# A cluster attention kernel: scores against the centroids from the tile of k and q, a transfer that adds, and a new order of the work

## The chip, the core and the metric

The kernel runs on one core of a Trainium2 chip. The metric is the device time of one execution in microseconds (us), the median of several runs of the same program.

## The reference

Attention over 32 heads (4 batches of 8) of 768 rows and 64 columns, in which a query sees only those keys that fall into its own cluster of 16; then a gated linear unit over the 512 columns of the 8 heads of a batch: a causal convolution of width 5 makes the gate.

```python
q_assign = np.argmax(np.einsum('bhsd,hcd->bhsc', q_n, c_n), axis=-1)
k_assign = np.argmax(np.einsum('bhsd,hcd->bhsc', k_n, c_n), axis=-1)
mask = q_assign[:, :, :, None] == k_assign[:, :, None, :]
scores = scale * np.matmul(q, k.transpose(0, 1, 3, 2))
scores = np.where(mask, scores, -1000000000.0)
attn = np.exp(scores - np.max(scores, axis=-1, keepdims=True))
attn = attn / (np.sum(attn, axis=-1, keepdims=True) + 1e-09)
x = np.matmul(attn, v)
# x as (batch, 768, 512), then
for k in range(5):
    gate_pre += conv_w[k][None, None, :] * xp[:, k:k + S, :]
out = (1.0 / (1.0 + np.exp(-gate_pre)) * (x @ w_val)) @ w_out
```

## The kernel before, in words

**Heads and tiles.** Heads are taken in 16 pairs. For a head, the scores stand transposed: a tile has 128 keys on the partitions and 768 queries along a row, so a head has 6 key tiles. Four matmuls make one (L614, L619): k and q are split into a high and a low part, and the two matmuls per half of the queries share one buffer `sp` of two in PSUM. The mask takes part in the matmul: 16 rows of the operands hold the cluster of each key and, times 2^100, that of each query, so that scores of other clusters come out far below zero. ScalarE takes the exponential of a tile (`expo`, L642) into one of 16 buffers `pt`, with a shift that VectorE finds from the head's first tile (L633, L637). TensorE multiplies v by the tiles of both heads of a pair (`av`, L759), 12 steps for a pair.

**Sums.** The denominator is the sum over all keys. VectorE first adds the six tiles of a head into one buffer `ad` of two (`add_p`, L213 by the helper `both`): five additions of 128x768 in f32 for each head. TensorE then sums over the partitions for both heads (`sum_p`, L685), which frees the two `ad`. ScalarE copies the sums out (L692), and after a reciprocal and a broadcast through DRAM VectorE scales the output of the pair by them (`scale_x`, L775).

**Clusters.** For each pair, four matmuls against the pair's centroids `cenT` (`prep_sims`, L489) make scores of k and q: 32 rows for each of four blocks. They read tiles `sraw` of their own, 128 x 384, with the 64 columns of both heads on the partitions (`load_sims`, L477). VectorE transposes, takes the largest and transposes back (L499, L510, L511, L512), TensorE finds the first of equal ones (L520), and ScalarE writes a row of ones and zeros (`prep_first2`, L524) and then the mask tile `oht` (`prep_oh`, L529), whose rows are moved to where the matmul operands need them (`prep_mask`, L575, L578). From pair 2 on, two pairs make one group: one `oht` of 768 columns serves four heads.

**Operands.** `load_both` (L415) brings k and q of one head into a tile `raw` of two, k on the even and q on the odd partitions. ScalarE or VectorE rounds to the high part (L217 or L219), VectorE subtracts (L213), and four moves between tiles of SBUF (L428) make four operands.

**The rest.** The weights are decoded from 64-bit floats by VectorE and ScalarE early on (L339 to L347). For each batch, the convolution (L790), the gate (L795), the value projection (`val`, L834, three matmuls a step) and the output projection (`proj`, L865) follow when the four pairs of that batch are through.

**The order.** Every engine has one queue in program order. The code makes a list of about 2,000 operations with what each has to follow and which buffer it takes, and a table of numbers (`PLAN`) gives the one order in which they are issued. An entry may name the engine (V or A) and a buffer's number; `w45` is 45 idle matmuls. All DMAs are issued by SyncE (SP). GpSimd has only work at the start and two instructions at the end.

## Time and profile before

| | us |
|---|---|
| median of 3 runs (461.29 to 463.9) | 463.62 |
| the profiled execution | 462.52 |
| its span, first to last instruction | 460.8 |
| VectorE busy | 408.2 |
| ScalarE busy | 289.2 |
| DMA, share of the 16 engines | 50.8% |

Busy time is the union of an engine's instructions. TensorE's matmuls overlap and their ends are modelled, so its busy share says only that it has something to do; the distance from start to start of two matmuls tells its pace. The span is 1.7 us shorter than the execution's time.

### The profile page before, as it was taken

The page shows a single profiled execution, that of the slowest core. Times are in us where ns is not written, and L with a number is a line of the kernel's source. Part 1 is how long each engine was busy: PE and PEld are TensorE (multiplying, and loading weights), DVE is VectorE, ACT ScalarE, POOL GpSimd, SP SyncE. Part 2 cuts the span into 40 slices and gives each one's busy share as a digit, 9 for nine tenths or more (in the row PEclk, how much of TensorE's full clock was granted, in tenths as well). Part 3 has the DMA queues.
Part 4 walks back from the last instruction along what each step waited for, and adds up shares of the span by engine and source line. Part 5 has one row for each costly group of instructions (what it writes and reads, how often), then busy time and mean ns, then how long its engine had stood idle before and what let it go on. Part 6 is the DMA issues. An engine that isn't in the chain of part 4 may idle for free. (4 is left out here: it accounts for less than half of the span.)

```text
span 460.8 us, 7572 instructions
## 1 busy us (share of the span) xinstructions
PE 448.9 (97%) x2655; PEld 322.1 (70%) x2655; DVE 408.2 (89%) x724; ACT 289.2 (63%) x428; POOL 6.0 (1%) x36
## 2 busy tenths in 40 slices
PE   7899999999999999999999999999999999999996
PEld 6655465655695868648496884958668696848985
DVE  5999899999999999999999798997988886788850
ACT  7968676969794776738964643756657454531521
POOL 4000000000000000000000000000000000000000
PEclk9999999999999999999999999999999999999999
DMA  8666786777567464366545643665435331200112
GB/s 250 219 197 211 226 263 195 245 236 241 174 208 238 142 212 147 126 191 200 181 148 184 215 135 123 183 192 190 158 122 183 133 101 58 68 15 1 70 48 94
DMA packets 39622, 75.17 MB, mean 163 GB/s; under 512 B 10652, under 2 KB 18716, under 8 KB 39580
## 3 DMA queue, kind: packets, MB, share of 16 engines
q1 hardware_dynamic: 39580, 74.65, 50.8%
q8 instruction: 22, 0.36, 0.3%
q14 instruction: 20, 0.16, 0.1%
HBM read 41.60 MB, written 6.38 MB: 104 GB/s over the span
## 5 line engine op out<-in xcount | busy, mean ns | idle before, releaser
L642 ACT ACTIVATE pt<-sp,sp 128x768 f32<-128x768 f32 x192 | 165.7, 901 | 64.9 <-DVE sp L637 25.5
L759 PE MATMUL acc<-pt,vt 128*64 128x384 f32 x768 | 130.0, 490 | 0.0
L213 DVE TENSOR_TENSOR ad<-ad,pt 128x768 f32<-128x768 f32 x128 | 119.9, 951 | 2.1
L614 PE MATMUL sp<-op,op 128*128 128x384 f32 x372 | 102.2, 355 | 3.0 <-ACT pt L642 2.3
L759 PEld LDWEIGHTS acc<-pt,vt 128*64 128x64 f32 x768 | 52.8, 137 | 67.4 <-issue 63.5
L619 PE MATMUL sp<-op,op 128*128 128x384 f32 (+1 forms) x372 | 95.4, 337 | 0.0
L614 PEld LDWEIGHTS sp<-op,op 128*128 128x128 f32 x372 | 63.3, 188 | 28.7 <-ACT pt L642 14.0
L790 DVE SCALAR_TENSOR_TENSOR gate<-xr,cw,gate 128x768 f32<-128x768 f32 (+1 forms) x84 | 67.9, 820 | 2.1 <-ACT gate L217 1.3
L619 PEld LDWEIGHTS sp<-op,op 128*128 128x128 f32 (+1 forms) x372 | 67.3, 188 | 0.2 <-issue 0.2
L865 PE MATMUL acc<-wh_o,h 128*128 128x512 f32 x144 | 50.3, 397 | 0.0
L834 PE MATMUL acc<-xh,wh_v 128*128 128x384 f32 x112 | 38.0, 340 | 0.0
L834 PE MATMUL acc<-xl,wh_v 128*128 128x384 f32 x112 | 37.8, 337 | 0.0
L834 PE MATMUL acc<-xh,wl_v 128*128 128x384 f32 x112 | 37.7, 337 | 0.0
L213 DVE TENSOR_TENSOR ad<-pt,pt 128x768 f32<-128x768 f32 x32 | 30.2, 944 | 2.2 <-ACT pt L642 2.2
L865 PEld LDWEIGHTS acc<-wh_o,h 128*128 128x128 f32 x144 | 27.1, 188 | 5.8 <-issue 0.6
L871 ACT ACTIVATE ob<-acc 128x512 f32<-128x512 f32 (+1 forms) x22 | 12.6, 576 | 29.1 <-PE acc L865 23.8
L213 DVE TENSOR_TENSOR op<-raw,op 128x768 fp32r<-128x768 f32 (+2 forms) x34 | 30.5, 902 | 0.1
L865 PE MATMUL acc<-wl_o,h 128*128 128x512 f32 x72 | 28.6, 397 | 0.0
L692 ACT ACTIVATE lr<-acc 128x384 f32<-128x384 f32 x16 | 7.9, 493 | 24.3 <-PE acc L685 18.5
L840 DVE SCALAR_TENSOR_TENSOR gate<-gate,acc 128x384 f32<-128x384 f32 x28 | 15.4, 549 | 8.6 <-PE acc L834 8.6
L217 ACT ACTIVATE op<-raw 128x768 fp32r<-128x768 f32 x26 | 21.9, 844 | 1.5 <-DMA raw<-kT 0.9
L834 PEld LDWEIGHTS acc<-xh,wh_v 128*128 128x128 f32 x112 | 21.0, 188 | 0.9 <-issue 0.6
(164 smaller groups left out, 490.8 us busy)
## 6 DMA issues: line engine op xcount, KB each, us to landing
op<-op SPq DMA_DIRECT2D x120, 192.0 KB, 2.5
raw<-kT SPq DMA_DIRECT2D x32, 192.0 KB, 3.4
raw<-qT SPq DMA_DIRECT2D x32, 192.0 KB
vt<-v SPq DMA_DIRECT2D x16, 384.0 KB, 4.4
out_dram<-ob SPq DMA_DIRECT2D x23, 256.0 KB, 2.2
sraw<-kT SPq DMA_DIRECT2D x30, 192.0 KB, 3.2
sraw<-qT SPq DMA_DIRECT2D x30, 192.0 KB, 3.8
rs<-rr SPq DMA_DIRECT2D x30, 192.0 KB, 3.3
```

Of the source, the lines that this page charges most:

```text
L213: (V if on[0] == "V" else G).tensor_tensor(out_, a, b, op=op)
L217: S.activation(out_, in_, AF.Copy, scale=x)
L614: PE.matmul(sp[:, hf, 0:HALF], x1[:, ts_], y1[:, hf * HALF:(hf + 1) * HALF], start=True, stop=False)
L619: PE.matmul(sp[:, hf, 0:HALF], x2[0:KR, ts_], y2[0:KR, hf * HALF:(hf + 1) * HALF], start=False, stop=True)
L642: S.activation(o.rearrange("p (a b) -> p a b", a=2), sp[:, :, 0:HALF], AF.Exp, bias=shift[h], scale=QS)
L692: S.activation(lr, lacc.pop(p)[:, 0:HALF], AF.Copy)
L759: PE.matmul(acc[e * D:(e + 1) * D, 0:HALF], vt[:, j, e * D:(e + 1) * D], pts[2 * p + e, j][:, hf * HALF:(hf + 1) * HALF], start=(j == 0), ...
L790: V.scalar_tensor_tensor(g, xr[:, k + c0:k + c1], cw[:, ct, k:k + 1], g, op0=ALU.mult, op1=ALU.add)
L834: PE.matmul(macc["v", b, ch, m][:, 0:HALF], a[:, kt, ms], x[:, kt, cs], start=(kt == 0 and i == 0), stop=(kt == NC - 1 and i == 2))
L840: V.scalar_tensor_tensor(gv, gv, 1.0, macc.pop(("v", b, ch, m))[:, 0:HALF], op0=ALU.add, op1=ALU.mult)
L865: PE.matmul(macc[b, ch, t, c0][:, 0:c1 - c0], x[kt][:, ts_], a[:, kt, c0:c1], start=(kt == 0 and i == 0), stop=(kt == NC - 1 and i == 2))
L871: S.activation(ob[:, 0:c1 - c0], acc[:, 0:c1 - c0], AF.Copy)
```

## The change

Scores against the centroids are taken from `raw`, the tile with k and q of one head on alternate partitions, and the tiles `sraw` with their 60 loads go. For that a second form of the centroids is made at the start: `cen2` has each centroid twice, once on the even partitions (zero on the odd) and once the other way, by one matmul of a copy `cen_d` and two scalings (`spread_cen`). The four blocks of scores are now two heads by two halves. Every pair is a group of its own, so `oht` has 384 columns, and a mask of a head takes two moves of half the width. `raw` has four buffers in place of two.

The last of the five additions of heads 0 to 11 is no longer VectorE's: GpSimd issues a transfer from the last `pt` to `ad` that adds to what is there (`add_last`). `PLAN` is another table.

```diff
@@ -263,6 +263,29 @@
             G.memset(t[r:r + C], 0.0)
 
 
+    oh_s2 = const.tile([P, 1], F32, name="oh_s2")
+    oh_b2 = const.tile([P, 1], F32, name="oh_b2")
+
+    def make_rows():
+        for t, x, y in ((oh_s2, BIG, 1.0), (oh_b2, -BIG, 0.0)):
+            G.memset(t, x)
+            for r in range(0, P, 32):
+                G.memset(t[r:r + C], y)
+
+
+    par = const.tile([P, 2], F32, name="par")
+    V.tensor_reduce(out=par, in_=ident.rearrange("p (a j) -> p j a", j=2), op=ALU.add, axis=AX.X)
+    cen2 = const.tile([P, HB, 2, C], F32, name="cen2")
+    cen_d = const.tile([P, D, 2], F32, name="cen_d")
+    cen_2 = []
+
+    def spread_cen(j):
+        if j is None:
+            cen_2.append(bank())
+            PE.matmul(cen_2[0][:, 0:P], cen_d.rearrange("p d j -> p (d j)"), ident, start=True, stop=True)
+        else:
+            scaled(cen2[:, :, j, :], cen_2[0][:, 0:P].rearrange("p (h c) -> p h c", c=C), par[:, j:j + 1])
+
     cen_f = const.tile([P, D], F32, name="cen_f")
     cenT = const.tile([P, NP, 2, C], F32, name="cenT")
     G.memset(cenT, 0.0)
@@ -298,7 +321,7 @@
             else:
                 S.activation(dst, src, AF.Copy)
 
-    oh = const.tile([P, SQ], BF16, name="oh")
+    oh = const.tile([P, HALF], BF16, name="oh")
 
 
     xrs = []
@@ -400,7 +423,7 @@
 
     def load_head(h, nm):
 
-        t = ring(raw_p, 2, [P, SQ], F32, "raw")
+        t = ring(raw_p, 4, [P, SQ], F32, "raw")
         src = kT if nm == "q" else qT
 
         for c in range(2):
@@ -410,7 +433,7 @@
 
     def load_both(h):
 
-        t = raws[h] = ring(raw_p, 2, [P, SQ], F32, "raw")
+        t = raws[h] = ring(raw_p, 4, [P, SQ], F32, "raw")
         for c, src in enumerate((kT, qT)):
             nc.sync.dma_start(out=t[c:P:2], in_=src[h])
 
@@ -429,7 +452,7 @@
 
     def clear(i):
 
-        z = cleared[i] = op_p.tile([P, SQ], F32R, name=f"op3_{i}", bufs=1)
+        z = operand(2 + i, 3)
         if i == 0:
             G.memset(z.bitcast(F32), 0.0)
         else:
@@ -461,35 +484,25 @@
 
 
 
-    groups = [[0], [1]] + [[p, p + 1] for p in range(2, NPAIR, 2)]
+    groups = [[p] for p in range(NPAIR)]
     group_of = {p: g for g, ps in enumerate(groups) for p in ps}
     ohts, sims, am, aeq, sraw = {}, {}, {}, {}, {}
-
-    def quads(g, r):
-        if len(groups[g]) > 1:
-            return [(p, j, r) for p in groups[g] for j in range(2)]
-        return [(groups[g][0], j, hf) for hf in range(2) for j in range(2)]
-
-    def load_sims(g, r, e):
-        p, j, hf = quads(g, r)[e]
-        t = sraw[g, r, e] = ring(am_p, 4, [P, HALF], F32, "sraw")
-        src = (kT, qT)[j][2 * p:2 * p + 2, :, hf * HALF:(hf + 1) * HALF]
-        nc.sync.dma_start(out=t, in_=src.rearrange("h d s -> (h d) s"))
 
     def load_first(j):
         t = pt_p.tile([P, SQ], F32, name=f"pt{NPT - 5 - j}")
         nc.sync.dma_start(out=t, in_=(kT, qT)[j][0:2].rearrange("h d s -> (h d) s"))
-        for e, (p, i, hf) in enumerate(quads(0, 0)):
-            if i == j:
-                raws[0, j, hf] = sraw[0, 0, e] = t[:, hf * HALF:(hf + 1) * HALF]
+        for hf in range(2):
+            raws[0, j, hf] = sraw[2 * hf + j] = t[:, hf * HALF:(hf + 1) * HALF]
+
 
     def prep_sims(g, r):
         acc = sims[g, r] = bank()
-        for e, (p, j, hf) in enumerate(quads(g, r)):
+        for e in range(4):
+            h, hf = 2 * g + e // 2, e % 2
             PE.matmul(
                 acc[32 * e:32 * e + 32, 0:HALF],
-                cenT[:, p % NP].rearrange("p h c -> p (h c)"),
-                sraw.pop((g, r, e)),
+                (cen2[:, h % HB] if g else cenT[:, 0]).rearrange("p h c -> p (h c)"),
+                raws[h][:, hf * HALF:(hf + 1) * HALF] if g else sraw[e],
                 start=True, stop=True, tile_position=(0, 32 * e),
             )
 
@@ -524,15 +537,16 @@
         S.activation(oh[:, r * HALF:(r + 1) * HALF], aeq.pop((g, r))[:, 0:HALF], AF.Relu)
 
     def prep_oh(g):
-        n = len(groups[g]) * HALF
-        oht = ohts[g] = am_p.tile([P, SQ], F32R, name="oht", bufs=1)
-        S.activation(oht[:, 0:n], oh[:, 0:n], AF.Identity, bias=oh_b, scale=oh_s)
+        oht = ohts[g] = am_p.tile([P, HALF], F32R, name="oht", bufs=1)
+        S.activation(oht, oh, AF.Identity, bias=oh_b2, scale=oh_s2)
 
     def operand(h, i):
 
         if h == 0:
             return pt_p.tile([P, SQ], F32R, name=f"pt{NPT - 1 - i}")
         if i == 3 and h > 1:
+            if h % 2 not in cleared:
+                cleared[h % 2] = op_p.tile([P, SQ], F32R, name=f"op3_{h % 2}", bufs=1)
             return cleared[h % 2]
         return op_p.tile([P, SQ], F32R, name=f"op{i}_{h % 2}", bufs=1)
 
@@ -564,18 +578,14 @@
         both(y2[0:D, c], raws["k", h][0:D, c], ops[h][2][0:D, c].bitcast(F32))
 
     def prep_mask(h, j):
-        g = group_of[h // 2]
-        oht, ps = ohts[g].bitcast(F32), groups[g]
+        oht = ohts[h // 2].bitcast(F32)
         dst = ops.setdefault(h, [None] * 4)
         if dst[1 + 2 * j] is None:
             dst[1 + 2 * j] = operand(h, 1 + 2 * j)
         dst = dst[1 + 2 * j][1:2 * C:2].bitcast(F32)
-        r = 64 * ps.index(h // 2) + 32 * j + C * (h % 2)
-        if len(ps) > 1:
-            nc.sync.dma_start(out=dst, in_=oht[r:r + C])
-        else:
-            for hf in range(2):
-                nc.sync.dma_start(out=dst[:, hf * HALF:(hf + 1) * HALF], in_=oht[r + 64 * hf:r + 64 * hf + C, 0:HALF])
+        for hf in range(2):
+            r = 64 * (h % 2) + 32 * hf + C * j
+            nc.sync.dma_start(out=dst[:, hf * HALF:(hf + 1) * HALF], in_=oht[r:r + C])
 
     def prep_mask0(h, i, hf, c0=0, c1=HALF):
 
@@ -670,6 +680,9 @@
             ads[h, g] = pt_p.tile([P, SQ], F32, name=f"ad{got[0]}")
         o = ads[h, g]
         both(o, pts[h, js[0]] if i == 1 else o, pts[h, js[i]], ALU.add)
+
+    def add_last(h, g, i):
+        G.dma_start(out=ads[h, g], in_=pts[h, GROUPS[h // 2][g][i]], accum_op=ALU.add)
 
     lacc, sums = {}, {}
 
@@ -886,7 +899,7 @@
     slot = {ht: s for s, ht in enumerate(tiles)}
 
 
-    RING = {"sp": 2, "raw": 2, "sraw": 4, "vt": 2, "rr": 2, "rs": 1, "lr": 1, "ob": 2, "oht": 1, "st": 2,
+    RING = {"sp": 2, "raw": 4, "vt": 2, "rr": 2, "rs": 1, "lr": 1, "ob": 2, "oht": 1, "st": 2,
             "wt": 2, "rc": 2, "shift": 3}
     POOL = {"pt": NPT, "ad": NAD, "acc": 4, "sq": 4}
 
@@ -930,7 +943,8 @@
             if t in js[1:]:
                 i = js.index(t)
                 src = [EX[slot[h, j]] for j in (js[:2] if i == 1 else js[i:i + 1])]
-                AD[h, g, i] = Op("AD", "V", add_p, h, g, i, after=src + [AD.get((h, g, i - 1))], take="ad" if i == 1 else None).frees(*src)
+                kind, eng, f = ("AG", "G", add_last) if i == NT - 1 and h < 12 else ("AD", "V", add_p)
+                AD[h, g, i] = Op(kind, eng, f, h, g, i, after=src + [AD.get((h, g, i - 1))], take="ad" if i == 1 else None).frees(*src)
 
 
     X2 = Op("X2", "A", prep_x2, 1)
@@ -957,9 +971,13 @@
     held("pt", NPT - 5).users = [x10, x11]
 
     ZM = {3: Op("ZM", "AV", clear, 1, after=[last_qk[1]])}
-    LT = None
+    LT, LTS = None, {}
     for h in range(2, NH):
-        LT = dma("LT", load_both, h, take="raw", after=[LT])
+        if h < 4:
+            LT = held("raw")
+        else:
+            LT = dma("LT", load_both, h, take="raw", after=[LT])
+        LTS[h] = LT
         war = [last_qk[h - 2]] if h > 2 else []
         XH = Op("XH", "AV", prep_hi, h, after=[LT] + war)
         XL = Op("XL", "V", prep_lo, h, after=[XH]).frees(LT)
@@ -971,19 +989,14 @@
         XHS[h] = XH
         low[h], ready[h] = [MC, *z], [XL, MA, MB, MC, MD]
 
-    am_, poh, prev = None, None, None
-    sraw1 = [held("sraw") for _ in range(4)]
-    for g in range(1, len(groups)):
-        np_ = len(groups[g])
+    C2 = Op("C2", "P", spread_cen, None, take="acc")
+    C3 = [Op("C3", "VA", spread_cen, j, after=[C2]).frees(C2) for j in range(2)]
+    am_, poh = None, None
+    for g in range(1, NPAIR):
         fr = []
-        for r in range(np_):
-            ls = sraw1
-            if g > 1:
-                ls = []
-                for e in range(4):
-                    prev = dma("LS", load_sims, g, r, e, take="sraw", after=[prev])
-                    ls.append(prev)
-            SI = Op("SI", "P", prep_sims, g, r, after=[] if g == 1 else ls, take="acc").frees(*ls)
+        for r in range(1):
+            ls = [LTS[2 * g], LTS[2 * g + 1]]
+            SI = Op("SI", "P", prep_sims, g, r, after=C3 + ls, take="acc").frees(*ls)
             AM = st_ = Op("AM", "V", prep_argmax1, g, r, after=[SI], take="st").frees(SI)
             for i in range(3):
                 AM = Op(("A1", "A2", "A3")[i], "V", prep_argmax2, g, r, i, after=[AM, am_])
@@ -1111,101 +1124,99 @@
 
 
     PLAN = """
-        0 3 1452 w45.0 801.0 582 583 576 578 577 1 579 589A 585A 591 4.0 581 2.1 588A 580 587A 584A 6 9 7.2 1540 586A
...
+        1415 577 591V 593 583 576 0 799.0 800A 3 1 1404 2.0 801V w7.2 802.2 982 589A 6 594 578 580 585A 4.1 581 588A
...
     """
 
     order, played, holds = [], set(), {}
@@ -1238,8 +1249,8 @@
     load_head(1, "k")
     load_conv()
     load_v(0)
-    for e in range(4):
-        load_sims(1, 0, e)
+    for h in (2, 3):
+        load_both(h)
     prep_cen()
     make_first()
     clear(0)
@@ -1252,6 +1263,8 @@
     lo0(1, 0, HALF)
     on[0] = "G"
     lo0(0, 0, 2 * P)
+    make_rows()
+    G.tensor_copy(cen_d, cen_f.unsqueeze(2).broadcast_to([P, D, 2]))
     on[0] = "A"
     for c in (0, HALF):
         copy0(1, c, c + HALF)
```

What the table does, at four places. First VectorE at the additions of pair 1 (heads 2 and 3: `ad_632` and `ad_729` before, `ad_656` and `ad_710` now). Before:

```order
90 L213 TENSOR_TENSOR ad_729<-ad_729,pt_742 128x768
91 L499 STREAM_TRANSPOSE st_762<-acc_746 128x384
92 L213 TENSOR_TENSOR ad_632<-ad_632,pt_685 128x768
93 L213 TENSOR_TENSOR ad_729<-ad_729,pt_744 128x768
94 L213 TENSOR_TENSOR xl<-xl,wh_v 128x512
95 L510 TENSOR_REDUCE amx_804<-st_762 128x24
96 L213 TENSOR_TENSOR wl_v<-xl 128x512
97 L213 TENSOR_TENSOR ad_729<-ad_729,pt_790 128x768
98 L775 TENSOR_TENSOR xr_123<-acc_538,rs_757 128x384
99 L213 TENSOR_TENSOR op_1_835<-raw_754,op_1_834 128x768
100 L775 TENSOR_TENSOR xr_123<-acc_534,rs_757 128x384
101 L213 TENSOR_TENSOR ad_729<-ad_729,pt_792 128x768
```

Now:

```order
84 L213 TENSOR_TENSOR ad_710<-pt_674,pt_686 128x768
85 L523 TENSOR_REDUCE amx_715<-st_695 128x24
86 L213 TENSOR_TENSOR ad_710<-ad_710,pt_705 128x768
87 L213 TENSOR_TENSOR ad_710<-ad_710,pt_726 128x768
88 L370 SCALAR_TENSOR_TENSOR xl<-xl 128x512
89 L213 TENSOR_TENSOR op_1_752<-raw_462,op_1_751 128x768
90 L213 TENSOR_TENSOR ad_710<-ad_710,pt_759 128x768
91 L524 TENSOR_TENSOR aeq_716<-st_695,amx_715 128x384
92 L643 TENSOR_REDUCE nm_776<-sp_766 128x1
93 L647 TENSOR_SCALAR sp_778<-nm_776 128x1
94 L213 TENSOR_TENSOR xl<-xl,wh_v 128x512
95 L788 TENSOR_TENSOR xr_129<-acc_522,rs_731 128x384
```

The fifth addition (of the tile `pt_792`, and of `pt_685` for head 2) is gone. Behind the fourth comes the shift of head 4 (`nm_776`, `sp_778`), which before stood behind the fifth.

These additions are now GpSimd's, in this order, the first two of pair 0, the next two of pair 1, then the first of pair 2 (each waits for the exponential of the tile that it reads and for the fourth addition):

```order
43 L685 DMA ad_385<-pt_498 128x768
44 L685 DMA ad_471<-pt_530 128x768
45 L685 DMA ad_656<-pt_650 128x768
46 L685 DMA ad_710<-pt_773 128x768
47 L685 DMA ad_862<-pt_836 128x768
```

TensorE ahead of the sums of pair 1 (L698 now, L685 before), behind the last two score tiles of head 4 (`sp_822`, `sp_831`):

```order
319 L624 MATMUL sp_822<-op_0_647,op_0_645 128x384 x2
320 L629 MATMUL sp_822<-op_0_232,op_0_646 128x384 x2
321 L533 LDWEIGHTS first
322 L533 MATMUL acc_827<-om_717,first 128x384
323 L624 MATMUL sp_831<-op_0_647,op_0_645 128x384 x2
324 L629 MATMUL sp_831<-op_0_232,op_0_646 128x384 x2
325 L698 MATMUL acc_843<-ad_710,wt_719 32x384
326 L698 MATMUL acc_843<-ad_656,wt_719 32x384
327 L698 MATMUL acc_843<-ad_710,wt_719 32x384
328 L698 MATMUL acc_843<-ad_656,wt_719 32x384
```

The sums read what the third and fourth of those transfers leave. Before, they stood behind head 4's first two score tiles; now they stand behind its sixth.

SyncE's queue in that part of the program, before:

```order
54 L428 DMA op_0_679<-op_0_679 64x768
55 L575 DMA op_0_680<-oht 16x768
56 L575 DMA op_0_228<-oht 16x768
57 L477 DMA sraw_817<-kT 128x384
58 L477 DMA sraw_819<-qT 128x384
59 L477 DMA sraw_821<-kT 128x384
60 L428 DMA op_1_564<-op_1_834 64x768
61 L428 DMA op_1_836<-op_1_835 64x768
62 L428 DMA op_1_836<-op_1_834 64x768
63 L477 DMA sraw_874<-qT 128x384
```

And now:

```order
37 L451 DMA op_0_647<-op_0_645 64x768
38 L451 DMA op_0_647<-op_0_646 64x768
39 L451 DMA op_0_232<-op_0_645 64x768
40 L588 DMA op_0_232<-oht 16x384 x2
41 L724 DMA rr_712<-rc_677 128x12
42 L588 DMA op_0_646<-oht 16x384 x2
43 L451 DMA op_0_645<-op_0_645 64x768
44 L731 DMA rs_731<-rr_712 64x768 x2
45 L451 DMA op_1_753<-op_1_751 64x768
46 L451 DMA op_1_535<-op_1_751 64x768
```

The loads of `sraw` are gone, and each mask (L575 before, L588 now) is two moves of half the columns.

## Rows read from the trace of the kernel before

**Rows 1.** The page: span, and busy us, share and instructions of two engines.

```profile
span 460.8 us, 7572 instructions
PE 448.9 (97%) x2655; PEld 322.1 (70%) x2655; DVE 408.2 (89%) x724; ACT 289.2 (63%) x428; POOL 6.0 (1%) x36
```

**Rows 2.** Stretch, length; busy PE, PEld, DVE, ACT, POOL; clock, DMA share, GB/s.

```profile
0.00:20.00 20.00, 16.51 (x164) 12.99 (x165) 14.69 (x43) 16.64 (x28) 4.88 (x34) 1.00 0.76 232
20.00:140.00 120.00, 116.94 (x680) 74.03 (x680) 117.26 (x205) 96.78 (x141) 0.00 (x0) 1.00 0.68 221
140.00:240.00 100.00, 98.98 (x579) 69.31 (x578) 97.28 (x168) 68.21 (x101) 0.00 (x0) 1.00 0.56 174
240.00:440.00 200.00, 200.00 (x1155) 152.07 (x1155) 174.73 (x302) 103.82 (x154) 1.08 (x2) 1.00 0.39 125
```

**Rows 3.** Waits from 20 to 140 us: who waited for whom, us, times, longest.

```profile
PEld sp L614 <- ACT pt L642: 11.7, 20, 0.9
ACT pt L642 <- DVE sp L637: 8.5, 5, 3.4
ACT pt L642 <- PE sp L619: 7.7, 10, 3.5
```

**Rows 4.** Groups by line and shape: busy us, mean ns of one, idle before.

```profile
L642 ACT ACTIVATE pt<-sp,sp 128x768 f32<-128x768 f32 x192 | 165.7, 901 | 64.9 <-DVE sp L637 25.5 <-PE sp L619 22.5 <-PE acc L759 14.3
L213 DVE TENSOR_TENSOR ad<-ad,pt 128x768 f32<-128x768 f32 x128 | 119.9, 951 | 2.1
L790 DVE SCALAR_TENSOR_TENSOR gate<-xr,cw,gate 128x384 f32<-128x384 f32 x40 | 24.0, 612 | 0.4
L775 DVE TENSOR_TENSOR xr<-acc,rs 128x384 f32<-128x384 f32 x30 | 16.2, 552 | 2.1 <-DMA rs<-rr 2.1
L499 DVE STREAM_TRANSPOSE st<-acc 128x384 f32<-128x384 f32 x16 | 9.2, 573 | 0.1
L219 DVE TENSOR_SCALAR op<-raw 128x768 fp32r<-128x768 f32 x5 | 2.8, 557 | 0.1
L219 DVE TENSOR_SCALAR gate<-xr,cw 128x384 f32<-128x384 f32 x4 | 1.7, 416 | 0.0
```

**Rows 5.** Order of time: start us, us, engine, line, operation, tiles, count.

```profile
10.42 0.69 DVE L594 TENSOR_SCALAR pt<-acc,oh_s,oh_b 16x384 fp32r<-16x384 f32 x1
11.80 2.69 PE L600 MATMUL acc<-idle 128*128 128x128 bf16 x45
22.59 1.82 DVE L213 TENSOR_TENSOR ad<-ad,pt 128x768 f32<-128x768 f32 x2
118.47 2.16 PE L759 MATMUL acc<-pt,vt 128*64 128x384 f32 x12
120.56 0.62 PE L614 MATMUL sp<-op,op 128*128 128x384 f32 x2
149.60 0.85 PE L685 MATMUL acc<-ad,wt 128*32 128x384 f32 x8
213.70 0.51 PE L619 MATMUL sp<-op,op 128*128 128x384 f32 x2
214.05 0.51 PE L614 MATMUL sp<-op,op 128*128 128x384 f32 x2
```

**Rows 6.** The tile of masks: duration ns min/median/max, first and last start.

```profile
L575 SPq DMA_DIRECT2D op<-oht x56: 513/564/1817, 48.5 to 383.0; - x56
L529 ACT ACTIVATE oht<-oh,oh_b,oh_s x8: 749/1026/1078, 24.0 to 340.0; 128x768 fp32r<-128x768 bf16 x7, 128x384 fp32r<-128x384 bf16 x1
L578 SPq DMA_DIRECT2D op<-oht x8: 544/584/590, 24.8 to 36.5; - x8
```

**Rows 7.** DMA issues on the page: count, KB each, median us from issue to landing.

```profile
op<-op SPq DMA_DIRECT2D x120, 192.0 KB, 2.5
vt<-v SPq DMA_DIRECT2D x16, 384.0 KB, 4.4
sraw<-kT SPq DMA_DIRECT2D x30, 192.0 KB, 3.2
```

186 lines of the change are left out of this document (92 added, 94 removed).

## The prediction, made before the changed kernel was run

> **What bounds the kernel now.** I read the page's busy shares first, then the busy time by stretch, then the waits of the stretch in which the engines are tightest. TensorE is busy 97% of the span and VectorE 89% [rows 1]. By stretch the two part [rows 2]: from 20 to 140 us VectorE works 117.26 of 120 us and TensorE shows 116.94; from 140 to 240 us VectorE has 2.7 us free and TensorE 1.0; from 240 to 440 us VectorE has 25 us free and TensorE none. The granted clock is 1.00 in all of them. ScalarE is at 81% in the first of these stretches and half idle in the last. What TensorE loses from 20 to 140 us shows better in its weight loads, since its matmuls overlap: the loads for the scores waited 11.7 us, in 20 places, for an exponential of ScalarE (it frees the buffer that the scores go to), and the exponentials waited 8.5 us for VectorE's shift and 7.7 us for TensorE [rows 3]. So up to about 150 us VectorE sets the pace and TensorE loses some 12 us; behind that TensorE has hardly a hole, and its work alone sets the end.
>
> **What the change takes away.** One of five additions of each of heads 0 to 11, an instruction of 0.951 us on VectorE [rows 4]. That is 12 x 0.951 = 11.4 us, all ahead of the sums of pair 5, which started at 149.6 us [rows 5], so all in the stretch that VectorE bounds.
>
> It isn't all gained. The plan is one list. Cut at the sums of pair 5, VectorE's part of it lacks the 12 additions and one transposition (0.57), and has more of these, by the rows of their shapes [rows 4]: three half steps of the convolution (0.61 each), its half-wide first step and half a scaling of v (0.42 each), a scaling of the output by the sums and a gate of the same width (0.55 each), two roundings to a high part (0.56 each), a mask of head 1 (0.69, by its like on VectorE [rows 5]), and half of the spread of the centroids over k and q, which no row shows (128 columns out of PSUM: between nothing and the 0.55 of 384 columns; I take 0.3). The extras make 5.9, so VectorE is relieved of 11.4 + 0.6 - 5.9 = 6.1 us. Two additions in a row take 1.82 us [rows 5], 0.91 each on the clock, so 6.1 us of durations are 5.8 on the clock. **First term:** the sums of pair 5 start at 143.8 us.
>
> **What is left behind that point.** TensorE's total hardly changes. 17 of 115 warm-up matmuls go (45 took 2.69 us [rows 5], so 1.0 us), and one small matmul comes to spread the centroids (between one warm-up's 0.06 us and the 0.35 of two score matmuls; I take 0.2). Ahead of the cut it also does four steps of attention times v less (12 matmuls, three steps, from 118.47 to 120.56 us: 0.7 each, 2.8 us) and four steps of the value projection more (three matmuls of the scores' width each, at 0.175 us from start to start [rows 5]: 2.1 us). So behind the cut, where it is the bound, it has 0.7 us more to do. **Second term:** +0.7. Together -5.1: 462.5 - 5.1 = 457.4 us against the profiled execution, whose span was 460.8 [rows 1]. The median of the runs shown, 463.6, is 1.1 above that execution, so the sum would read 458.5 from there. I say 457.8, between the two.
>
> **What costs nothing, and under what cover.**
> The score matmuls against the centroids read the tile of k and q that is loaded anyway; they are as many and as wide as before. The 60 second loads of 192 KB go, 11.8 MB [rows 7]. The DMA engines were at 0.68 from 20 to 140 us [rows 2], and no wait for such a load stands among the long ones, so a lighter queue is worth nothing by itself.
> ScalarE writes fifteen half tiles of masks where it wrote seven whole ones and a half: 15 x 0.75 against 7 x 1.03 + 0.75 [rows 6], 3.3 us more, and hands some copies to VectorE (counted above). It had 23 us free from 20 to 140 us. Without that cover a late exponential would cost TensorE its 0.90 us [rows 4].
> GpSimd gets two rows of constants and one broadcast copy at the start. It had nothing to do from 20 us on and 15 us free before. A delay there would hold up the scores of pair 1 against the centroids, and with them its masks.
>
> **The transfer that adds** is the unknown; nothing in the trace adds in flight. The nearest rows: moves within SBUF, 192 KB, land in 2.5 us, and a load of 384 KB in 4.4 [rows 7]. The transfer writes 384 KB and reads 768, so its price lies between 2.5 us and twice 4.4 = 8.8. I take 5: near the row of its size, with something for the second read. TensorE's sums wait for it, and behind them all of TensorE's queue. For pair 1 TensorE has 8.2 us of work, by the paces of rows 5, between the scores of the last key tile and the sums (the order above shows the end of it); the exponential takes 0.90 of it. For pairs 0 to 5, taking VectorE's fourth addition where that comes later, the cover is 5.9, 7.3, 7.6, 8.4, 11.0 and 7.9 us. At 5 us nothing waits. At 8.5 us the waits are 2.6 + 1.2 + 0.9 + 0.1 + 0.6 = 5.4 us and the gain is gone.
> One rule speaks against the change. In the trace a rounding on VectorE over 128x768 takes 0.56 us where an addition of that width takes 0.95 [rows 4], so VectorE has a faster mode for some instructions; GpSimd issues no transfer beside it, so no row shows whether the two disturb each other. The Trainium skill ("SBUF — State Buffer", Who interferes with whom) says that in a two-port mode VectorE holds a pair of ports which GpSimd needs to write a transfer's descriptors, for the whole instruction, and that an ordinary addition doesn't hold up those writes. By it a transfer would at times be held for one such rounding, 0.56 us, and 5.6 us is still under the smallest cover; several in a row would lead to the late transfer below.
>
> **The rivals.**
> *TensorE's work is the whole bound.* For it: 97% busy, and a plan that fills holes with later work. Then only its own sum counts, -1.0 + 0.2: 461.7 us. Against it: 11.7 us of waiting in the weight loads, in the very stretch where VectorE has no hole.
> *The masks come late.* Each pair now has its own chain: a half tile on ScalarE and four issues on SyncE for a head, 0.75 + 4 x 0.58 = 3.1 us, where four heads shared one of 1.03 + 2 x 0.56 = 2.2 us [rows 6]. If 6 of 14 pairs paid that difference of 0.9 us, 5.4 us would go: 462.8. For it: the plan leaves TensorE only 5.2 to 10 us of work between a pair's mask and its scores, and the chain with the landing is near 6. Against it: the scores of half of the heads, the second of each pair, have 12 us and more.
> *The transfer lands late.* Place: the sums of pairs 0, 1, 2, 3 and 5. Up to 5.9 us it costs nothing, at 8.5 us the time is that of before, and from 9.6 us on (3.7 + 2.3 + 2.0 + 1.2 + 1.7 = 10.9 us of waits) it is slower by over 1%: 468.3 us. For it: two reads, DMA engines at 0.68, a queue that GpSimd has to feed. Against it: the bound of 8.8 us from the rows.
> *More is won than VectorE gives.* A new order also moves the exponentials. If TensorE's 11.7 us of waits for them shrank to 1, 462.5 - 10.7 = 451.8. Against it: VectorE still has 111 of the 120 us to do.
>
> **How the numbers follow.** The forecast, a gain of 3 to 7.5 us (455 to 459.5): 0.48. TensorE alone, late masks, or transfers that land in 6 to 9 us (459.5 to 466): 0.30. Transfers later than that: 0.11. More than forecast (below 455): 0.11. About 1%, 4.6 us, is what a measurement of this kernel can tell from no change; the limits are 459.0 and 468.3. Faster takes five sixths of the forecast's case and all of the last: 0.51. Slower is most of the late transfer: 0.09. The same gets 0.40. The range goes from 451.8 (the waits gone), rounded to 451.5, to 465.5 (transfers at the bound of 8.8 us, whose waits of 7 us make 464.4, and 1.1 for the median).
>
> **What the changed profile would show.** Right: VectorE still without holes from 20 to 140 us, the sums of pair 5 starting near 144 us, the score loads' wait for ScalarE halved, the transfers landing within 6 us, TensorE without holes behind 150 us. The first term is wrong if pair 5's sums start later than 147 us while VectorE shows gaps; the second if TensorE loses over 3 us behind 150 us; the cover is wrong if the sums wait for a transfer, or the scores for the transfers of the masks.

## The result, and the profile after

| | before | changed |
|---|---|---|
| median us (7 runs each, same chip) | 463.32 | 467.63 |
| lowest to highest | 461.29 to 464.49 | 466.12 to 469.39 |
| profiled execution, us | 462.52 | 468.38 |
| its span | 460.8 | 466.7 |

The changed kernel is a little slower: its time is 1.0099 of the time before, with a 95% interval of 1.0072 to 1.0126, or 4.6 us more. The forecast was 457.8 us, and its range ended at 465.5.

The page of the changed kernel, against [rows 1]: busy us and share of each engine (PE is TensorE, PEld its weight loads, DVE VectorE, ACT ScalarE, POOL GpSimd, SP SyncE), and the queue of the transfers (packets, MB, share of 16 DMA engines).

```profile
PE 451.9 (97%) x2640; PEld 320.8 (69%) x2640; DVE 402.3 (86%) x717; ACT 292.1 (63%) x433; POOL 17.7 (4%) x59
q0 software_dynamic: 1728, 4.72, 5.6%
```

VectorE has 5.9 us less to do, as the change intends, and TensorE is no better off for it. Busy time in two of the four stretches, with the columns of [rows 2]:

```profile
20.00:140.00 120.00, 115.44 (x663) 72.11 (x662) 112.31 (x204) 94.96 (x137) 8.74 (x10) 1.00 0.69 198
240.00:440.00 200.00, 199.06 (x1155) 148.58 (x1154) 170.73 (x296) 110.56 (x163) 1.22 (x2) 1.00 0.33 109
```

From 20 to 140 us VectorE is 5.0 us emptier, but TensorE has lost 1.5 us as well. The DMA engines stand at 0.69, where they stood at 0.68, although 60 loads are gone. The waits of that stretch, against [rows 3]:

```profile
PEld sp L624 <- ACT pt L652: 12.0, 21, 1.0
ACT pt L652 <- DVE sp L647: 9.9, 10, 2.5
ACT pt L652 <- PE sp L629: 6.5, 13, 1.7
```

The forecast had the first of them halved; it is as long as it was, and the other two have hardly changed in sum (16.4 us for 16.2). Two places in order of time: a score tile that waits for the masks, and the sums of pair 5, which stood at 149.60 us [rows 5].

```profile
41.37 0.59 PE L624 MATMUL sp<-op,op 128*128 128x384 f32 x2 [1.77 <-DMA op<-oht]
152.42 0.83 PE L698 MATMUL acc<-ad,wt 128*32 128x384 f32 x8
```

The transfers themselves did what was forecast: twelve issues of about 0.85 us on GpSimd, which land in 3.9 to 5.6 us. Here is the issue row of the page, and the last row of the view of tile `ad`:

```profile
ad<-pt POOLq DMA_DIRECT2D x12, 384.0 KB, 4.8
DMA to landing us min/median/max: 3.9/4.8/5.6
```

### The profile page after: what moved, and what is told of

It is laid out like the page before. It is cut to its first block, busy times and chain, and to the rows that moved or that the text cites. A ratio compares the mean times of both kernels' runs of the same rounds, so it can differ in the third digit from the quotient of the medians.

```text
span 466.7 us, 7606 instructions
## 1 busy us (share of the span) xinstructions
PE 451.9 (97%) x2640; PEld 320.8 (69%) x2640; DVE 402.3 (86%) x717; ACT 292.1 (63%) x433; POOL 17.7 (4%) x59
## 3 DMA queue, kind: packets, MB, share of 16 engines
q0 software_dynamic: 1728, 4.72, 5.6%
## 5 line engine op out<-in xcount | busy, mean ns | idle before, releaser
L213 DVE TENSOR_TENSOR ad<-ad,pt 128x768 f32<-128x768 f32 x116 | 109.0, 951 | 2.5
L624 PEld LDWEIGHTS sp<-op,op 128*128 128x128 f32 x372 | 62.1, 188 | 29.7 <-ACT pt L652 13.4
L884 ACT ACTIVATE ob<-acc 128x512 f32<-128x512 f32 (+1 forms) x22 | 12.7, 576 | 25.5 <-PE acc L878 20.5
L217 ACT ACTIVATE xh<-xr 128x768 fp32r<-128x768 f32 (+1 forms) x16 | 10.9, 684 | 17.1 <-DVE xr L786 7.4
L537 ACT ACTIVATE oh<-acc 128x384 bf16<-128x384 f32 x15 | 7.3, 488 | 22.6 <-PE acc L533 22.6
L217 ACT ACTIVATE op<-raw 128x768 fp32r<-128x768 f32 x22 | 18.5, 841 | 4.5 <-PE sp L624 4.5
```

Source lines behind the costliest of these rows:

```text
L213: (V if on[0] == "V" else G).tensor_tensor(out_, a, b, op=op)
L217: S.activation(out_, in_, AF.Copy, scale=x)
L537: S.activation(oh[:, r * HALF:(r + 1) * HALF], aeq.pop((g, r))[:, 0:HALF], AF.Relu)
L624: PE.matmul(sp[:, hf, 0:HALF], x1[:, ts_], y1[:, hf * HALF:(hf + 1) * HALF], start=True, stop=False)
L884: S.activation(ob[:, 0:c1 - c0], acc[:, 0:c1 - c0], AF.Copy)
```

## The experiments

Theory A is the forecast's: VectorE bounds the front, and something in the new order ate the gain. Theory B: VectorE never bounded it, so there was nothing to gain, and the new order costs. A third came up on the way: the transfers disturb what lands beside them.

All times are medians of several runs beside runs of the kernel before on the same chip. Rows with different times of the kernel before are compared by their ratios; 0.001 is 0.46 us.

| kernel | us | before | ratio (95%) | against before, us |
|---|---|---|---|---|
| old order, 12 additions left out | 461.11 | 461.71 | 0.9979 (0.9956 to 1.0002) | -1.0 |
| old order, 12 more operations | 473.69 | 462.26 | 1.0259 (1.0238 to 1.0280) | +12.0 |
| old order, 12 additions by transfer | 487.75 | 461.71 | 1.0553 (1.0523 to 1.0582) | +25.5 |
| old order, 12 transfers beside all additions | 473.84 | 462.35 | 1.0254 (1.0220 to 1.0288) | +11.7 |
| changed kernel again | 466.56 | 462.26 | 1.0103 (1.0082 to 1.0125) | +4.8 |
| new order, additions on VectorE | 471.80 | 461.71 | 1.0213 (1.0195 to 1.0231) | +9.8 |
| new order, 12 additions left out | 462.89 | 461.71 | 1.0024 (1.0012 to 1.0036) | +1.1 |
| new order, 12 plain transfers instead | 463.96 | 462.26 | 1.0043 (1.0022 to 1.0063) | +2.0 |
| new order, 5 of 12 transfers | 464.00 | 462.35 | 1.0044 (1.0026 to 1.0062) | +2.0 |
| new order, 12 adding transfers, unread | 472.14 | 462.35 | 1.0205 (1.0172 to 1.0238) | +9.5 |
| changed kernel, last groups swapped | 466.31 | 462.26 | 1.0098 (1.0076 to 1.0119) | +4.5 |
| the same, and the gate earlier | 468.16 | 462.35 | 1.0135 (1.0109 to 1.0161) | +6.2 |
| changed kernel, four waits covered | 465.60 | 461.79 | 1.0061 (1.0037 to 1.0086) | +2.8 |

### What VectorE's 11.4 us are worth

The first experiment gives the relief without any of its costs:

```diff
-AD[h, g, i] = Op("AD", "V", add_p, h, g, i, ...)
+f = (lambda *_: None) if i == NT - 1 and h < 12 else add_p
+AD[h, g, i] = Op("AD", "V", f, h, g, i, ...)
```

> The kernel before in its old order, with the fifth addition of heads 0 to 11 left out and nothing in its place (the row sums of these heads therefore miss one of six key tiles). It is the change's relief of VectorE, 12 x 0.95 = 11.4 us, without any of its costs. Theory A (the forecast's: VectorE's instruction stream sets the pace to 150 us): the sums of pair 5 start 6 to 11 us before their 149.6 us, and the run is 5 to 10 us shorter, about 453 to 458 us. Theory B (VectorE's high busy share there is no bound; the alternation of TensorE's score tiles, ScalarE's exponentials and two score buffers sets the pace): the sums of pair 5 start less than 2 us earlier and the run is within 2 us of 463 us; VectorE shows the 11 us as idle time.

It measured -1.0 us. Windows and waits of this kernel from 20 to 140 us, and its sums of pair 5:

```profile
20.00:140.00 120.00, 118.19 (x690) 75.89 (x689) 111.25 (x199) 98.64 (x142) 0.00 (x0) 1.00 0.70 224
...
ACT pt L642 <- DVE sp L637: 12.0, 6, 3.4
PEld sp L614 <- ACT pt L642: 11.5, 20, 0.8
DVE nm L633 <- PE sp L619: 3.2, 4, 1.3
...
148.17 0.85 PE L685 MATMUL acc<-ad,wt 128*32 128x384 f32 x8
```

The sums start 1.43 us earlier, not 6 to 11. VectorE is still busy for 111 us: it takes up later work earlier, and now waits itself for TensorE's scores (3.2 us, a wait that the kernel before does not have). The weight loads' wait for the exponentials is 11.5 us in 20 places, as in [rows 3]: it was never VectorE's. The opposite dose:

```diff
     both(o, pts[h, js[0]] if i == 1 else o, pts[h, js[i]], ALU.add)
+    if i == NT - 1 and h < 12:
+        both(o, o, o, ALU.max)
```

> The kernel before with VectorE's work increased by what the change takes away: the fifth addition of heads 0 to 11 is followed by one more operation of the same shape (the maximum of the tile with itself, which changes nothing), 12 x 0.95 = 11.4 us ahead of 150 us. Taking these 11.4 us away was worth 1.0 us. If VectorE has slack in the old order (TensorE's tiles and ScalarE's exponentials set the pace): +0 to +3 us. If the old order is packed right up to VectorE's work, so that less gains nothing but more costs, as the new order showed (8.9 us for the same 11.4): +6 to +11 us.

It measured +12.0 us: the whole 11.4 and a little more. From 20 to 140 us:

```profile
20.00:140.00 120.00, 111.24 (x627) 67.31 (x627) 117.31 (x197) 87.92 (x126) 0.00 (x0) 0.99 0.64 203
```

VectorE is as busy as before, and TensorE falls back by 5.7 us. So the two are level in the old order. VectorE bounds it upwards; downwards the bound is TensorE's own work in that order, only 1.0 us lower: without the additions TensorE is busy for 118.19 of the 120 us.

### The change, taken apart

Each part was taken back or made alone: the transfers put into the old order (with `add_last` as in the change), the additions put back into the new one, and both left out.

```diff
-kind, eng, f = ("AG", "G", add_last) if i == NT - 1 and h < 12 else ("AD", "V", add_p)
+kind, eng, f = "AD", "V", add_p                                          # additions on VectorE
+kind, eng, f = ("AD", "V", lambda *_: None) if i == NT - 1 and h < 12 else ("AD", "V", add_p)   # left out
```

> The kernel before in its old order, with the fifth addition of heads 0 to 11 done by the accumulating transfer: the second part of the change alone. The old order leaves 0 to 2 tiles of TensorE work between the second head's last addition and the pair's sums, so TensorE waits about 4 us (0.85 to issue plus 4.8 to land, less the 0.95 of the addition) in up to six pairs. Theory A: 6 x 4 = up to 24 us of waits, less up to 10 us of relief on VectorE, so +5 to +14 us. Theory B: no relief, +10 to +24 us, less what slack TensorE's queue has over the others; the sums of pairs 0 to 5 show the waits for the transfer.

It measured +25.5 us, above both. The sums' idle time by the view of line L688 (the sums in this kernel), and three of fifteen windows of 15 us from 20 to 245 us:

```profile
  DMA ad<-pt: 18.9, 9
...
110.00:125.00 15.00, 12.92 (x54) 6.65 (x54) 6.18 (x12) 6.86 (x10) 0.00 (x0) 0.67 0.59 171
140.00:155.00 15.00, 12.13 (x58) 10.01 (x57) 8.39 (x14) 8.90 (x13) 0.00 (x0) 0.77 0.66 196
170.00:185.00 15.00, 10.67 (x57) 7.45 (x54) 6.42 (x16) 4.05 (x6) 0.00 (x0) 0.77 0.59 149
```

The waits are there, 18.9 us in the records of weight loads and matmuls together, which overlap. The clock comes on top: in the stretch in which the sums waited 3.1 and 1.5 us, around 110 us, the mean granted clock is 0.67, that is, for about two thirds of the stretch the lower of the two levels (1.2 in place of 2.4 GHz). It is 0.77 in the stretches with a wait of 2.9 us for a mask (at 144 us) and of 4.3 us for a transfer (at 176 us), 0.89 in the one with a wait of 2.3 us (at 88 us), and 0.99 or more in the other eleven. No expectation had that. In the changed kernel no matmul waits that long, and the clock stays at 1.00.

> The changed kernel in its new order and with its new cluster scores, but with all five additions of heads 0 to 11 back on VectorE, at the places in the order where the transfers stood. Theory A: VectorE has 11.4 us more before 150 us, so +5 to +11 us over the changed kernel (473 to 479 us). Theory B: VectorE takes them in its idle time, 0 to +3 us (467 to 471 us). A third theory, that the transfers themselves disturb other transfers and hold the masks and raw tiles back: 2 to 5 us shorter than the changed kernel (463 to 466 us).

> The changed kernel without the fifth addition of heads 0 to 11 and without the transfers in its place (the row sums of these heads miss one of six key tiles). Theory A with transfers that are hidden: no change, 467 to 468 us. Theory B: no change either, within 1 us. The third theory, that the transfers delay others or the sums: 3 us or more shorter, 464 us or less; the masks' wait at 39 us and the raw tile's at 97 us, 1.9 and 1.1 us in the changed kernel, then go away.

The additions back on VectorE cost 5.2 us over the changed kernel (1.0213 against the mean of its two ratios, 1.0101). Without additions and without transfers the new order takes 1.0024: 3.6 us (within about 1.0) less than the changed kernel, and 2.1 us (within 1.2) more than the old order without additions. So neither theory holds alone. In the new order too VectorE bounds upwards, 8.7 us for 11.4; and the transfers, whose results nobody waits for, cost 3.6 us, as the third theory had it. So the loss has three parts: -1.0 for the relief, +2.1 for the new scores and order, +3.6 for the transfers. (Their sum, +4.7, is no check: each part is the difference of two neighbours on the way from the kernel before to the changed one.)

### Why transfers that nobody waits for cost 3.6 us

The changed kernel once more, as the reference:

> The changed kernel itself once more, as the reference for the three beside it on the same chip, and as a second profile. If the 1.0 us by which its first score matmuls stood behind in the first profile (first load landing at 7.0 us, in three other kernels at 6.0 to 6.7) is chance, it goes away or changes here; the waits for masks at 41 us, for a raw tile at 97 us and behind the row sums' row at 125 us (1.9, 1.1 and 1.0 us) stay. Time 4 to 5 us over the kernel before.

A part of the 1.0 us at the start was chance: the scores that wait for the first load now start at 6.46 us, in the first profile at 7.05. The masks' wait at 41 us, here at 40, fell from 1.77 to 0.94 us. The other two stayed, at 1.1 and 0.7 us. TensorE executes the same matmuls in the same order in this kernel and in the one without transfers, so their start times can be compared one by one. The place of the raw tile, first without transfers, then with them (rows in order of time):

```profile
89.50 0.60 SPq L438 DMA_DIRECT2D raw<-qT  x1
93.00 0.85 PE L502 MATMUL acc<-raw,cen 128*32 128x384 f32 x8
```

```profile
90.83 0.85 POOL L685 DMA_DIRECT2D ad<-pt  x1 [6.53 <-ACT xh L217]
91.08 0.59 SPq L438 DMA_DIRECT2D raw<-kT  x1
91.73 0.59 SPq L438 DMA_DIRECT2D raw<-qT  x1
92.43 1.47 SPq L451 DMA_DIRECT2D op<-op  x1
94.44 0.84 PE L502 MATMUL acc<-raw,cen 128*32 128x384 f32 x4
96.35 0.84 PE L502 MATMUL acc<-raw,cen 128*32 128x384 f32 x4 [1.07 <-DMA raw<-qT]
```

Without transfers the scores start 3.5 us after the raw load was issued, and do not wait. With a transfer (that of head 7) 0.25 us ahead of the loads they wait until 4.6 us after it. The first half of them stands 1.4 us behind the kernel without transfers (94.44 against 93.00), the second half 3.0 (96.35 against 93.34). At 124 us it is a score tile behind two transfers (heads 8 and 9, issued at 114.68 and 116.14 us); the profile names a copy of ScalarE, which had ended 0.6 us earlier, so a move or a mask is the likely one.

The masks at 40 us are another matter. Without any transfer the score tile waits there too, and also in a kernel below that keeps the transfers of heads 2 to 6 alone, the first of them issued at 43 us:

```profile
39.26 0.58 PE L624 MATMUL sp<-op,op 128*128 128x384 f32 x2 [0.69 <-DMA lsum<-lr]
```

```profile
40.26 0.59 PE L624 MATMUL sp<-op,op 128*128 128x384 f32 x2 [0.92 <-DMA lsum<-lr]
```

The profile names the transfer of the sums, `lsum`, which a score tile doesn't read; a mask or a move issued beside it is the likely one. So of the 0.94 us about a quarter at most is the transfers' (the expectation that it goes away without them failed), and how much of the 1.77 us of the first profile is theirs stays open. What of the cost is traffic, and what the adding:

```diff
-    G.dma_start(out=ads[h, g], in_=pts[h, GROUPS[h // 2][g][i]], accum_op=ALU.add)
+    G.dma_start(out=ring(dr_p, 12, [P, SQ], F32, "junk"), in_=pts[h, GROUPS[h // 2][g][i]])
```

> The changed kernel with the twelve accumulating transfers replaced by twelve plain transfers of the same 384 KB from the same tiles at the same places, into memory that nothing reads (the row sums of heads 0 to 11 so miss one of six key tiles). Nobody waits for them. Without any transfer this kernel took 3.5 us less than the changed one. If the transfers' traffic beside the masks and raw tiles is the cause: no change from the changed kernel, within 1.5 us, and the masks at 41 us and the raw tile at 97 us are waited for again. If the row sums' wait for the addition is the cause: 3 us or more shorter than the changed kernel, as without transfers.

It measured +0.9 us (within about 1.1) over none, 2.7 under the changed kernel, between the two answers: the bytes sent are not the measure. The queue's share, the landing, and the stretch from 20 to 140 us of the kernel with plain transfers; then that stretch without transfers, and in the changed kernel run again:

```profile
q0 software_dynamic: 960, 4.72, 2.7%
junk<-pt POOLq DMA_DIRECT2D x12, 384.0 KB, 3.6
20.00:140.00 120.00, 118.55 (x683) 75.33 (x682) 115.92 (x208) 97.05 (x140) 6.68 (x12) 1.00 0.62 209
```

```profile
20.00:140.00 120.00, 118.94 (x690) 76.50 (x689) 116.64 (x210) 96.68 (x139) 0.00 (x0) 1.00 0.51 173
```

```profile
20.00:140.00 120.00, 116.45 (x670) 73.14 (x668) 113.45 (x204) 95.31 (x137) 8.73 (x10) 1.00 0.69 198
```

For the same 4.72 MB the adding transfers hold the DMA engines twice as long (5.6% against 2.7%). The new scores and order had brought the share from 0.68 down to 0.51; plain transfers bring it to 0.62, adding ones back to 0.69, and TensorE's busy time falls: 118.94, 118.55, 116.45. To see whether it is the traffic or a dependence on its result, the same adding transfers went into a buffer in memory that nothing reads:

```diff
+    scratch = dr_p.tile([P, SQ], F32, name="scratch")
+    def add_scratch(h, g, i):
+        src = pts[h, GROUPS[h // 2][g][i]]
+        if h: G.dma_start(out=scratch, in_=src, accum_op=ALU.add)
+        else: G.dma_start(out=scratch, in_=src)
```

> The changed kernel with its transfers replaced by accumulating transfers of the same tiles at the same places into one buffer in memory that nothing reads (the first of them a plain one; the row sums of heads 0 to 11 so miss one of six key tiles). Plain transfers of the same bytes cost 0.9 us over none at all and took 2.7 % of the DMA engines' time, the accumulating ones 5.6 % and 3.5 us. If it is the accumulating traffic beside masks, moves and raw tiles: within 1 us of the changed kernel (2.5 to 4 us over no transfers), and its share of the DMA engines' time is near 5 % again. If it is the row sums' or the buffers' dependence on the transfer: no more than the plain ones, 463.5 to 464.5 us.

> The kernel before, with all its additions, and beside them the twelve accumulating transfers into a buffer that nothing reads, at the places of the fifth additions of heads 0 to 11. Its DMA engines have a share of 0.68 from 20 to 140 us without them (in the new order without transfers 0.51). If the traffic slows what lies beside it whatever the order: +3 to +8 us, more than in the new order since more lies beside it. If only the new order's tight masks and raw tiles suffer: less than +1.5 us.

Both cost much more than expected: 8.4 us over none in the new order, 11.7 in the old. The queue in the new order:

```profile
q0 software_dynamic: 1664, 4.72, 6.0%
scratch<-pt POOLq DMA_DIRECT2D x12, 384.0 KB, 5.7
```

So adding transfers that nothing reads cost time in either order: no sum has to wait for them, and the new order isn't specially tight. Nor do VectorE and ScalarE work more slowly in the changed kernel: an addition takes 951 ns there and an exponential 898, against 951 and 901 [rows 4]. Why adding in memory costs 8.4 us and adding on the chip 3.6 isn't settled. The share of the DMA engines doesn't tell: from 20 to 140 us it is 0.66 here and 0.69 in the changed kernel. These transfers also stand in line for one buffer, and in this trace VectorE waits in three places for the sums on their way through memory, 6.7 us from 20 to 140 us, where the changed kernel run again has no such wait:

```profile
DVE rc L726 <- DMA lsum<-lr: 6.7, 3, 3.3
```

Then only some of the transfers:

```diff
-... ("AG", "G", add_last) ...
+... ("AG", "G", add_last if 1 < h < 7 else lambda *_: None) ...
```

> The changed kernel with only the transfers of heads 2 to 6; those of heads 0, 1 and 7 to 11 are left out (their row sums miss one of six key tiles). Place by place, TensorE lost nothing beside the transfers of heads 2 to 6, and 0.4 to 1.1 us at 40 us (heads 0 and 1), 1.2 to 2 us at 96 us (head 7), 0.9 us at 124 us (heads 8 and 9) and 0.5 us at 160 us (heads 10 and 11). If the cost lies in these collisions: within 1 us of no transfers at all, 2.5 us or more under the changed kernel. If each transfer costs the same: 5/12 of 3.5, so 1.5 us over no transfers and 2 us under the changed kernel.

It measured 0.9 us over none. Collisions alone had said under 1, an equal price 1.5; with an uncertainty of about 1.0 the time is on the side of the collisions, but doesn't decide. The trace says more. At the place of the raw tile this kernel issues the same loads within 0.05 us of the changed kernel run again, and of the transfers near it only that of head 7 is missing:

```profile
91.68 0.60 SPq L438 DMA_DIRECT2D raw<-qT  x1
92.39 0.53 SPq L451 DMA_DIRECT2D op<-op  x1
94.44 1.12 PE L502 MATMUL acc<-raw,cen 128*32 128x384 f32 x8
```

The scores start in both at 94.44 us. Here all eight matmuls are through within 1.12 us; beside the transfer the last four start only at 96.35, and the move behind the loads takes 1.47 us to issue, here 0.53. The sums of pairs 2 and 3, on either side of that place, in the changed kernel run again, in this one, and without any transfer:

```profile
75.41 0.85 PE L698 MATMUL acc<-ad,wt 128*32 128x384 f32 x8
98.71 0.85 PE L698 MATMUL acc<-ad,wt 128*32 128x384 f32 x8
```

```profile
75.78 0.85 PE L698 MATMUL acc<-ad,wt 128*32 128x384 f32 x8
97.09 0.85 PE L698 MATMUL acc<-ad,wt 128*32 128x384 f32 x8
```

```profile
74.34 0.85 PE L698 MATMUL acc<-ad,wt 128*32 128x384 f32 x8
95.40 0.85 PE L698 MATMUL acc<-ad,wt 128*32 128x384 f32 x8
```

The distances are 23.3, 21.3 and 21.1 us (23.3 in the changed kernel's first profile too). So beside one transfer of twelve, that of head 7, 2.0 us are lost, over half of the 3.6. The wait at 124 us is gone as well in the kernel without the transfers of heads 8 and 9.

### Where the new order loses 2.1 us

Two places stand behind the front: TensorE waits for a gate at 433 us, and a 512-wide and a 256-wide copy stand behind the last matmuls where one of 0.4 us stood.

```diff
 last groups:  -2029.1 2030 2031 2032 2033 2034 2018 2019 2023.3 2024 2020 2025 2021 2022 2026 ...
               +2018 2019 2020 2021 2022 2029.1 2030 2031 2032 2033 2034 2023.3 2024 2025 2026 ...
 gate earlier: -1913V 1914 1924 1925 1926 1904 1912 1952 2004.3 1983.1 1941 2005
               +1913V 1914 1941 1924 1925 1926 1904 1912 1952 2004.3 1983.1 2005
```

> The changed kernel with the last groups of the output projection in another order: the second of the two 512-wide groups is ended before the two 256-wide halves, as in the kernel before, so that one 256-wide copy of 0.4 us stands behind the last matmul in place of a 512-wide and a 256-wide one (1.1 us). If the new order's end is a part of the loss: 0.7 to 1.2 us shorter than the changed kernel; if the end is hidden in the last stores: within 0.3 us.

> The changed kernel with two places near its end in another order: the gate's multiplication for the first group of values is put ahead of three of the convolution's steps on VectorE (TensorE waits 1.4 us for it at 433 us), and the second 512-wide output group ends before the two 256-wide halves (0.3 us in the run before). If the end is part of what the new order costs: 1.2 to 2 us shorter than the changed kernel, 1.006 to 1.007 of the kernel before. If the wait only moves on to the next group: within 0.5 us of it.

The swap of the last groups alone gave 0.2 us, under what can be told. With the gate ahead it came out 1.5 us slower than the changed kernel (within about 1.4), a miss. The gate's operation and TensorE's wait, in the changed kernel run again and in this one:

```profile
433.30 0.55 DVE L853 SCALAR_TENSOR_TENSOR gate<-gate,sp 128x384 f32<-128x384 f32 x1
433.90 0.45 PE L847 MATMUL sp<-xh,wh_v 128*128 128x384 f32 x1 [0.94 <-DVE gate L853]
```

```profile
432.76 0.55 DVE L853 SCALAR_TENSOR_TENSOR gate<-gate,sp 128x384 f32<-128x384 f32 x1
433.36 0.44 PE L847 MATMUL sp<-xh,wh_v 128*128 128x384 f32 x1 [1.89 <-DVE gate L853]
```

The gate reads one half of a buffer, and matmuls write the other half. With the gate ahead of them in the program, they too had to wait for it. The last run puts the gate behind those matmuls but ahead of the convolution's steps, and covers three more waits:

```diff
 raw tile at 96 us:  -862.3 156 985 1511A 854 159 1089.0       +156 985 1511A 854 159 862.3 1089.0
 moves at 124 us:    -198 1114.2 1115                          +1114.2 198 1115
 gate at 433 us:     -1924 1925 1926 1904 1912 1952 2004.3 1983.1 1941 2005
                     +1904 1912 1952 2004.3 1983.1 1941 1924 1925 1926 2005
 (and the last groups as above)
```

> The changed kernel with the work that waits moved later, and the transfers as they were. (1) On TensorE the scores of pair 6 against the centroids stand two score tiles later, behind the place at 96 us where they waited 1.1 us for a raw tile that lands beside a transfer; (2) the sums of pair 4 stand ahead of the first score tile of head 11, which waited 0.7 us at 124 us for moves and masks beside two transfers; (3) the gate's multiplication at 433 us stands ahead of three steps of the convolution on VectorE, now behind the matmuls that share its buffer; (4) the 512-wide output group ends before the 256-wide halves. If the losses are local waits with work at hand to cover them: 1.2 + 0.7 + 1.4 + 0.3 = 3.6 us, at least 2 us, shorter than the changed kernel (1.002 to 1.006 of the kernel before). If each wait only moves on: within 1 us of the changed kernel (1.008 to 1.012).

It measured 1.0061, 1.9 us (within about 1.5) shorter than the changed kernel: a part comes back, about half of what the waits summed to. In its trace the waits at 124 and 433 us and for the raw tile are gone; a wait of 1.2 us at 92 us came anew. So at least some of the loss is local waits.

How the 2.1 us of the new order and scores divide was not tested by an edit. The two profiles without additions divide them by place. The sums of pair 5 start at 148.17 us in the old order, and in the new one without transfers here:

```profile
147.10 0.83 PE L698 MATMUL acc<-ad,wt 128*32 128x384 f32 x8
```

The new order is 1.1 us ahead there; from there to the end it takes 313.6 us (460.7 - 147.10) against 310.2 (458.4 - 148.17). So its loss lies behind pair 5, 3.4 us, of which the forecast's count of work moved there makes 0.7, and it needs no transfer. By the windows of the same two kernels TensorE is busy for 0.4 us less in the first 20 us of the new order (16.41 against 16.81), 0.8 us more from 20 to 140 us, and 0.9 us less from 240 to 440 us (199.06 against 200.00). No version beats the kernel before by a difference that can be measured: even with the additions left out the old order gains only 1.0 us.

## Why the prediction was wrong

**What bounds the kernel.** Half right. VectorE bounds the stretch to 150 us in that more work there costs its full time (12.0 us for 11.4). It doesn't follow that less work gains; that was the reading that failed. "TensorE loses some 12 us" took the waits of the weight loads for lost time. A weight load waits while the matmuls ahead of it still run. The row of the stretch had the bound in it: TensorE was busy for 116.94 of 120 us [rows 2], so it had 3.1 us to give back, not 12, and without the additions it gave back 1.4.

**First term, the sums of pair 5 at 143.8 us: the step that failed.** They came at 152.42. The forecast priced 6.1 us less work on VectorE at 5.8 us on the clock; the old order, with 11.4 us less of it and all its other work unchanged, gained 1.0 (1.4 at this place in the profile).

**Second term, +0.7 us behind that point: too small.** From the sums of pair 5 to the end of the span it was 311.2 us before (460.8 - 149.60) and 314.3 after (466.7 - 152.42): +3.1, and +3.4 without additions and transfers. The wait for the gate is 1.4 us of it by its weight load; the last copies looked like 1.0, but the swap showed that little of that comes back.

**What costs nothing.** Here the second failed step lies. The lighter DMA queue was priced at nothing, and the twelve transfers were weighed only against the sums that read them. What else lands beside them, the moves, masks and raw tiles of the next heads, had no price: 3.6 us. The new work at the start shows as 0.4 us less busy time in the first 20 us; in the same kernel's two profiles the landing of the first load alone moved the scores that wait for it by 0.6 us.

**The transfer's price.** Right: 5 us taken, 4.8 measured, and the covers of 5.9 to 11 us held; no sum waited for a transfer from 20 to 165 us. That it came so near is in part luck, since the rows only bounded it between 2.5 and 8.8. On the rule of the Trainium skill ("SBUF — State Buffer", Who interferes with whom), that a two-port instruction of VectorE can hold up GpSimd's descriptors: issues took 0.84 to 1.02 us and landings 3.9 to 5.6, with no delay long enough to matter; the trace doesn't tell more.

**The rivals.** "TensorE's work is the whole bound" was the right account of the relief: it gave less work on VectorE nothing, and 1.0 us was measured. (Its number, 461.7 us, is no support: the 0.8 us that it gains are fewer warm-up matmuls, which the old order keeps.) "The masks come late" was seen at one place, at 40 us: 0.7 us without transfers, 0.9 and 1.8 in the two profiles with them. "The transfer lands late" carried the chance of slower, and did not happen. Its own ground, that transfers share engines which are at 0.68, was right, but the ones to come late were the others. "More is won" fell.

## What to carry to other kernels

When two engines are busy for 98% of a stretch, taking work from one gains at most what the other has idle; read that from the other's row before pricing the relief, and don't add up waits that overlap with running work. A transfer that nobody waits for isn't free: price what is issued and lands beside it, place by place, and ask who waits for that. When the old order was made for the old work, an experiment that leaves the work out in that order gives the ceiling of the whole idea.

## What the runs showed of the hardware

An adding transfer of 384 KB inside SBUF lands in 4.8 us (median of 12); twelve of them held the DMA engines for 5.6% of the span. Plain ones of the same bytes to memory landed in 3.6 us and held them for 2.7%, adding ones to memory in 5.7 and for 6.0%. Beside an adding transfer the issue of moves and masks on SyncE's queue itself can take longer: 1.47 us against 0.53 for the move at 92 us, and for four masks beside the transfers of heads 8 and 9, in the changed kernel run again and in the one without these two:

```profile
115.88 4.01 SPq L588 DMA_DIRECT2D op<-oht  x4
```

```profile
114.53 2.46 SPq L588 DMA_DIRECT2D op<-oht  x4
```

Not every slow issue is due to a transfer: two masks at 30 us took 2.78 us in the changed kernel and 1.14 without transfers, but 2.03 with the transfers of heads 2 to 6 alone, the first of which was issued 13 us later.

And long waits of TensorE went with a loss of clock: in the old order with transfers the granted clock was 0.89, 0.67, 0.77 and 0.77 in the four stretches of 15 us with waits of 2.3 us and more. Multiplied by 15 us, what is missing to 1.00 makes 13.5 us, an estimate and an upper one of what the clock cost, since TensorE also waited in these stretches. The changed kernel, in which no matmul waited longer than 1.8 us, kept 1.00.
